# Attention block with a gated feed-forward on one core: weight preparation spaced wider, and the DMA queue reordered

## The chip, the cores and the metric

The kernel runs on one core of one Trainium2 chip. The metric is the time of one execution in device microseconds (us); lower is better. Before the change the median of three runs is 1711.38 us (1709.61 to 1713.75).

## What is computed

One transformer block in float32 with 2048 rows of 512 values. The modulation rows `sa, ca, ga, sb, cb, gb` are six slices of `silu(c) @ w_mod`.

```
h = layernorm(x) * (1 + ca) + sa
q = h @ wq  (32 heads of 16);  k = h @ wk, v = h @ wv  (one shared head of 16)
p = softmax(q @ k^T / 4);  o = p @ v
x = x + ga * (o @ wo)
h = layernorm(x) * (1 + cb) + sb
out = x + gb * (((h @ w_gate) * (h @ w_up)) @ w_down)      (inner width 1792)
```

Products whose inputs are not small are made from float16 halves: a value is scaled, rounded to float16 (the high half), and the rest is kept as a second float16 value (the low half). Three matmul terms then replace one. Each weight matrix needs a scale for that, and the scale comes from a bound on the size of its entries.

## The kernel before

**Units, turns, steps.** The attention runs in 32 units u. A unit is one block of 256 rows (eight blocks) and one group of 8 heads (four groups). It has 16 key tiles kt; the work of one kt is called a turn here. A turn has two steps, so unit u has the steps 32u to 32u+31. In a turn TensorE makes four score tiles `sc` (line 647, `qk_exp`), ScalarE turns them into `P` by exp (line 649), and TensorE adds `P` times the values into `pv` (line 658). Each turn also makes the row maxima of a unit one ahead: score tiles `mx` (line 592) whose maxima VectorE takes (line 596). VectorE and ScalarE therefore have one fixed load per turn, and four exp instructions mark one turn in the trace.

**Side work.** TensorE's remaining time in a turn goes to groups of "side" matmuls (line 502), taken in order from a list `fill`: first 16 projections of q (`q_proj`), then for each block of 256 rows the output product (`wo_work`), the gate and up products and the down product (`ffn_work`). A turn with a q projection takes in fewer side matmuls (called a thin turn here, order `FEW`) than one with later groups (a full turn, order `MANY`). Thin turns are nearly all of the steps 0 to 156 and 172 to 192; the rest are full. Which style a turn has is fixed when the program is written out, and so is the order on every engine; each engine runs its own list strictly in order.

**Weight preparation.** `late_weights` makes a list of items, and `side_step` issues one item when its gap in steps since the last one is over. `stage` loads one piece of a weight (224 or 256 KB) from HBM into one of three buffers `wsl`. `norms` squares the pieces on GpSimd and adds them up by column (`square`, lines 928 and 930); `sums` adds the columns over partitions with a matmul (line 940). `gcols` to `last_inverse` make scales from the maxima. `split` and `pipelined` load the pieces a second time, scale them on GpSimd and write the two halves (lines 1044 to 1052). The order before is: norms of `wo`, `w_gate`, `w_up`; their scales; the split of those three; norms of `w_down`; its scale; its split.

**The queue.** Nearly every DMA is issued by SyncE (SP), one after the other, and an issue that has to wait holds all behind it. The list of SP holds: the loads of weight pieces (line 921), which wait until GpSimd has released one of the three buffers; the writes of the q halves (line 540), which wait for GpSimd; the loads of a unit's q halves into `sst` (`load_q`, line 557); the row maxima `mt` of a unit (line 630), which its first score tile needs; at each unit's end (`pv_out`) eight small copies of the output `ev` to `oc` and two of the row sums to `rs` (lines 672, 674); the steps of `normalise`, that is the load `rc` of the row sums (line 682), VectorE's reciprocal (line 685), its write `ri` and its broadcast load `rr` (lines 687, 689); the rows of x for the residual (line 719).

**Normalisation.** `hooks` runs the three parts of `normalise(u - 1)` in unit u at the steps 5 (load), 10 (reciprocal on VectorE, in line with the maxima) and 15 (product and halves on GpSimd, lines 694 to 697). After every fourth unit it puts the output product and the feed-forward groups into `fill`.

Of the kernel before, what the change touches and what calls it, by code (L numbers as in the profile page):

```python
# [25 lines left out]
NC = KC  # L26
# [30 lines left out]
def adaln_mqa_glu_kernel(ctx: ExitStack, tc: tile.TileContext, x_in, wq_in, wk_in, wv_in, wo_in,  # L57
# [473 lines left out]
    def q_proj(b, ch):  # L531

        def evac(p):
            q16 = work.tile([128, 2, BT], F16, name="q16", tag="ev", bufs=3)
            qf = work.tile([128, BT], F32, name="qf", tag="ev", bufs=3)
            nc.scalar.activation(qf, p, AF.Copy, scale=qvs[:, 0:1])
            nc.gpsimd.tensor_scalar(q16[:, 0, :], qf, 1.0, 0.0, op0=OP.mult, op1=OP.add)
            nc.gpsimd.tensor_tensor(q16[:, 1, :], qf, q16[:, 0, :], op=OP.subtract)
            d = dram.tile([128, 2, BT], F16, name=f"qd{b}_{ch}")
            nc.sync.dma_start(d, q16)  # L540
# [120 lines left out]
    def pv_out(u):  # L661
        sb, ch = divmod(u, NC)
        ev = work.tile([128, BT], F32, name="ev", tag="ev", bufs=3)
        nc.scalar.activation(ev, pvb[u], AF.Copy, scale=evs)
        ps_give(pvb[u])
        oc[u] = work.tile([128, ST], F32, name="oc", tag="oc", bufs=2)
        rsum[u] = dram.tile([8, ST], F32, name=f"rs{u}")
        for c in range(2):
            for j in range(4):
                p, a = divmod(j, 2)  # L670
                r = 16 * (4 * p + 2 * c + a)
                nc.sync.dma_start(oc[u][r:r + 16, :], ev[32 * j:32 * j + 16, c * ST:(c + 1) * ST])  # L672
        for p in range(2):
            nc.sync.dma_start(rsum[u][4 * p:4 * p + 4, :].rearrange("(c a) n -> a c n", a=2),
                              ev[64 * p + 16:64 * p + 64:32, :].rearrange("a (c n) -> a c n", c=2))

    def normalise(u):
        st = {}
# [34 lines left out]
    xls = {}  # L713
    n2s = {}
    n2f = {}

    def load_x(t):
        xl = work.tile([128, D], F32, name="xl", tag="xl", bufs=3)
        nc.sync.dma_start(xl, x_rows[t * 128:(t + 1) * 128, :])
        xls[t] = xl  # L720

    def wo_work(sb):
        on_pool = 2 <= sb < NS - 2

        def op(t):
            def f(i):
                ch, term = divmod(i, 3)
                ol, wl = TERMS[term]
                return [(och[sb, ch][:, ol, t * 128:(t + 1) * 128], wo[:, wl, ch, :])]
            return f  # L730

        def fin(t):
            row = 2 * sb + t

            def f(p):
                if sb < NS - 1:
                    x1 = work.tile([128, D], F32, name="x1", tag="x1", bufs=6)
                else:
                    x1 = work.tile([128, D], F32, name="x1p", tag="P", bufs=8)
                nc.vector.scalar_tensor_tensor(x1, p, sca[:, 7:8], xls[row], op0=OP.mult, op1=OP.add)  # L740
                x1s[row] = x1
# [142 lines left out]
    def late_weights():  # L884
# [30 lines left out]
        items = []  # L915
        sl = list(wslices())
        gm = work.tile([128, 4], F32, name="gm", bufs=1)

        def stage(n):
            t = work.tile([128, D], F32, name="wsl", tag="xl", bufs=3)  # L920
# [26 lines left out]
        def norms(order):  # L947
            ns = [n for m in order for n in range(len(sl)) if sl[n][0] == m]
            out = []
            waiting = deque()  # L950
            for j in range(len(ns) + 2):
                def f(j=j):
                    if j < len(ns):
                        stage(ns[j])
                    if j >= 2:
                        square(ns[j - 2])
                out.append((SQ_GAP, nothing, f))
                if waiting:
                    out.append((0.5,) + sums(*waiting.popleft()))
                m = sl[ns[j - 2]][0] if j >= 2 else None  # L960
                if m is not None and (j == len(ns) + 1 or sl[ns[j - 1]][0] != m):
                    waiting.extend((m, n) for n in range(4))
            out.append((SUM_GAP, nothing, nothing))
            return out + [(2,) + sums(*w) for w in waiting]

        def gcols():
            nc.vector.tensor_reduce(cmx[:, 0:4], cmq, axis=AX.X, op=OP.max)
# [40 lines left out]
            nc.gpsimd.tensor_scalar(gab, gab, sca[:, 3:4], 0.0, op0=OP.mult, op1=OP.add)  # L1008

        def last_column():  # L1010
            nc.vector.tensor_reduce(cmx[:, 2:3], cmq[:, 2], axis=AX.X, op=OP.max)

        def last_scale():
            t = work.tile([128, 2], F32, name="scd", bufs=1)
# [37 lines left out]
                nc.gpsimd.tensor_tensor(wt[:, 1, i, c], t, wt[:, 0, i, c], op=OP.subtract)  # L1052
            return load, gate, halves

        def pipelined(ns):
            sp = [split(n) for n in ns]
            out = []
            for n in range(len(ns) + 2):
                def f(n=n):
                    if n >= 2:  # L1060
                        sp[n - 2][2]()
                    if n < len(ns):
                        sp[n][0]()
                    if 1 <= n <= len(ns):
                        sp[n - 1][1]()
                out.append((SPLIT_GAP, nothing, f))
# [5 lines left out]
        items += norms((2,)) + [(1, nothing, last_column), (2, tr, trp), (3, bc, last_scale), (1, nothing, last_inverse)]  # L1072
        return items, pipelined(list(range(n2, len(sl)))), [m0(k) for k in range(KC)] + [m1, m2, m3]

    def run_items(items):
        for _, f, post in items:
# [168 lines left out]
    def hooks(u, i):  # L1245
        step = u * NSTEP + i
        if later_h and i % 2 and i > 4:
            b1, k = later_h.popleft()
            h_halves(b1, (k,))
        side_step(step)  # L1250
        if u > 0 and i in (5, 10, 15):
            if i == 5:
                nrm[:] = normalise(u - 1)
            nrm[(5, 10, 15).index(i)]()
        if i == 16 and u > 0 and u % NC == 0:
            sb = u // NC - 1
            left = list(fill)
            fill.clear()
            gu, down = ffn_work(sb)
            early = max(len(left) - LATE_Q, 0) if sb == 0 else min(len(left), 2)  # L1260
            fill.extend(left[:early])
            fill.extend(([step + (6 if sb == 0 else 4)], w) for w in wo_work(sb))
            fill.extend(left[early:])
            fill.extend((["h2", sb], w) for w in gu + down)

# [77 lines left out]
```

## Time and profile before

| | |
|---|---|
| median of three runs | 1711.38 us |
| the profiled execution | 1711.02 us |
| its span, first to last instruction | 1708.9 us |
| TensorE busy | 1665.0 us (97%) |
| VectorE, ScalarE, GpSimd busy | 1404.0, 1232.1, 553.0 us |
| mean granted TensorE clock | 0.988 |
| TensorE busy from 80 to 517 us | 409.0 of 437 us, clock 0.96 |
| TensorE busy from 517 to 1600 us | 1080.7 of 1083 us, clock 1.00 |

The profiled execution takes 2.1 us more than its span and stands 0.4 us under the median. Names in the profile: PE is TensorE, PEld its weight loads, DVE VectorE, ACT ScalarE, POOL GpSimd, SP SyncE, and SPq a DMA issue on SP's queue. L596 is line 596. "A <- B" in a list of waits says that an instruction of A sat idle until B; the numbers are us in total, how many times, and the longest. In a table of windows each row is a stretch of the span, then its length, then busy us with the count of instructions, then the granted clock.

### The profile page before, as it was taken

How to read it: one execution, taken by the hardware profiler on the slowest of the kernel's cores; microseconds unless marked ns; L12 is line 12 of the kernel's file. 1: busy time of each engine (PE TensorE's matmuls, PEld its weight loads, DVE VectorE, ACT ScalarE, POOL GpSimd, SP SyncE). 2: the span in 40 equal slices, each digit the busy share in tenths (PEclk: the TensorE clock that was granted, in tenths of full speed). 3: DMA queues.
4: the chain of work that ended last, by engine and by line, in shares of the span. 5: the costliest groups of instructions: out<-in, count | busy, mean ns of one | idle time of the engine just before them, and what ended most of it. 6: DMA issues, size and time to landing. Idle time of an engine off the chain costs nothing.

```text
span 1708.9 us, 39953 instructions
## 1 busy us (share of the span) xinstructions
PE 1665.0 (97%) x15648; PEld 750.1 (44%) x15648; DVE 1404.0 (82%) x2438; ACT 1232.1 (72%) x2361; POOL 553.0 (32%) x860
## 2 busy tenths in 40 slices
PE   8988999999999999999999999999999999999999
PEld 4322232235543355434544345443545335453776
DVE  7988998789979899989999999989998999880211
ACT  5667787677867787777787777777778777787300
POOL 5766758785750111110113011310113101210322
PEclk9899999999999999999999999999999999999999
DMA  7122323331211000000000000000000000000000
GB/s 251 71 76 87 91 62 99 99 91 50 77 32 31 19 13 14 25 18 12 13 19 17 19 19 13 25 14 19 20 24 6 13 23 19 19 8 15 26 13 13
DMA packets 66024, 67.27 MB, mean 39 GB/s; under 512 B 21542, under 2 KB 50730, under 8 KB 65836
## 3 DMA queue, kind: packets, MB, share of 16 engines
q1 hardware_dynamic: 63724, 64.15, 12.4%
q8 instruction: 122, 2.00, 0.5%
q10 hardware_dynamic: 2112, 0.59, 0.1%
q14 instruction: 66, 0.54, 0.1%
HBM read 51.32 MB, written 8.92 MB: 35 GB/s over the span
## 4 chain that ended last, share of the span: by engine, by line
PE 78%; DVE 5%; POOL 4%; DMA 4%; SPq 3%; ACT 3%; issue 1%; ACTq 0%; POOLq 0%; DVEq 0%
PE side L502 35%; PE pv L658 25%; PE sc L647 9%; PE mx L592 7%; DVE mpart L596 4%; SPq L672 2%; ACT P L649 2%; DMA rc<-rs 1%; DMA rs<-ev 1%; DMA wsl<-in_B_w_up_dram 1%; POOL kwb L930 1%; PE mx L796 1%; POOL wsl L1050 1%; DMA xbig<-in_A_x_dram 1%; POOL wsl L928 0%
## 5 line engine op out<-in xcount | busy, mean ns | idle before, releaser
L596 DVE TENSOR_REDUCE mpart<-mx 128x1 f32<-128x512 f32 x2016 | 1274.1, 684 | 113.8 <-PE mx L592 98.1
L649 ACT ACTIVATE P<-sc 128x512 f32<-128x512 f32 x2048 | 1099.1, 599 | 317.5 <-PE sc L647 238.5
L647 PE MATMUL sc<-sst,kst 50*128 50x512 f16 (+1 forms) x2297 | 699.9, 357 | 9.1 <-DMA sst<-mt 5.1
L592 PE MATMUL mx<-kst,sst 48*128 48x512 f16 x2032 | 640.6, 380 | 12.8 <-DVE mpart L596 7.9
L658 PE MATMUL pv<-P,vst 128*32 128x512 f32 x4096 | 550.6, 610 | 0.6
L502 PE MATMUL side<-h2T,wg 64*128 64x256 f16 (+1 forms) x2372 | 536.5, 271 | 0.2 <-ACT P L649 0.2
L502 PE MATMUL side<-h2T,wu 64*128 64x256 f16 (+1 forms) x2372 | 534.8, 270 | 0.0
L502 PEld LDWEIGHTS <-wg 64*128 64x128 f16 (+1 forms) x2372 | 224.1, 95 | 222.3 <-ACT P L649 183.9
L502 PE MATMUL side<-wd,glu 64*128 64x512 f16 (+1 forms) x1166 | 267.7, 378 | 0.4 <-ACT P L649 0.4
L841 POOL TENSOR_SCALAR glu<-gf 128x256 f16<-128x256 f32 x112 | 45.3, 405 | 659.0 <-DVE gf L840 612.2
L647 PEld LDWEIGHTS <-kst 50*128 50x128 f16 x2297 | 209.9, 94 | 88.7 <-issue 64.8
L502 PEld LDWEIGHTS <-wu 64*128 64x128 f16 (+1 forms) x2372 | 224.4, 95 | 49.1 <-issue 12.3
L592 PEld LDWEIGHTS <-sst 48*128 48x128 f16 x2064 | 191.6, 95 | 37.0 <-issue 14.4
L502 PEld LDWEIGHTS <-glu 64*128 64x128 f16 (+1 forms) x1166 | 97.1, 95 | 194.3 <-ACT P L649 87.7
L658 PEld LDWEIGHTS pv<-P,vst 128*32 128x32 f32 x4096 | 81.1, 108 | 164.8 <-issue 154.3
L840 DVE TENSOR_TENSOR gf<-side,g 128x256 f32<-128x256 f32 x112 | 46.7, 418 | 76.6 <-ACT g L838 68.0
L502 PE MATMUL side<-h,wq 64*128 64x512 f16 (+1 forms) x372 | 99.5, 382 | 0.5 <-ACT P L649 0.4
L838 ACT ACTIVATE g<-side 128x256 f32<-128x256 f32 x112 | 42.4, 379 | 72.3 <-PE side L502 70.6
L502 PE MATMUL side<-wo,och 64*128 64x512 f16 (+1 forms) x360 | 88.0, 382 | 0.1
L694 POOL TENSOR_TENSOR oc<-oc,rr 128x256 f32<-128x256 f32 x31 | 22.6, 729 | 176.8 <-DMA sst<-qd 131.7
L842 POOL TENSOR_TENSOR glu<-gf,glu 128x256 f16<-128x256 f32 x112 | 75.3, 672 | 9.4
L502 PEld LDWEIGHTS <-och 64*128 64x128 f16 (+1 forms) x360 | 30.8, 95 | 68.7 <-ACT P L649 30.2
(230 smaller groups left out, 814.2 us busy)
## 6 DMA issues: line engine op xcount, KB each, us to landing
wsl<-in_B_w_gate_dram SPq DMA_DIRECT2D x32, 224.0 KB
wsl<-in_B_w_up_dram SPq DMA_DIRECT2D x32, 224.0 KB
wsl<-in_B_w_down_dram SPq DMA_DIRECT2D x28, 256.0 KB
sst<-qd SPq DMA_DIRECT2D x180, 32.0 KB
qd<-q SPq DMA_DIRECT2D x16, 256.0 KB
oc<-ev SPq DMA_DIRECT2D x256, 16.0 KB
rr<-ri SPq DMA_DIRECT2D x32, 128.0 KB
xl<-in_A_x_dram SPq DMA_DIRECT2D x16, 256.0 KB
```

Of the source, the lines that this page charges most:

```text
L502: return nc.tensor.matmul(self.p[:, c * w:(c + 1) * w], left[rows], right[rows], start=start and c == 0, stop=stop and c == len(terms) - 1)
L592: nc.tensor.matmul(m, s[64 * a:64 * a + 48, p, t * 128:(t + 1) * 128], w[64 * a:64 * a + 48, :], start=(i == 0), stop=(i == len(keys) - 1))
L596: nc.vector.tensor_reduce(part, m, axis=AX.X, op=OP.max)
L647: nc.tensor.matmul(t[:, c0:c1], kst[64 * a:64 * a + 50, kt * 128:(kt + 1) * 128], s[64 * a:64 * a + 50, p, c0:c1], start=True, stop=True)
L649: ex = nc.scalar.activation(ptl[u, kt, p, a], t, AF.Exp)
L658: nc.tensor.matmul(pvb[u][32 * j:32 * j + 32, :], vst[:, kt, :], ptl[u, kt, p, a], start=(kt == 0), stop=(kt == KT - 1))
L672: nc.sync.dma_start(oc[u][r:r + 16, :], ev[32 * j:32 * j + 16, c * ST:(c + 1) * ST])
L694: eng.tensor_tensor(o, o, st["r"], op=OP.mult)
L838: nc.scalar.activation(g, p[:, 0:ST], AF.Copy, scale=2.0 ** -45)
L840: nc.vector.tensor_tensor(gf, p[:, ST:2 * ST], g, op=OP.mult)
L841: nc.gpsimd.tensor_scalar(glu()[:, 0, f, :], gf, 1.0, 0.0, op0=OP.mult, op1=OP.add)
L842: nc.gpsimd.tensor_tensor(glu()[:, 1, f, :], gf, glu()[:, 0, f, :], op=OP.subtract)
```

## The change

Weight preparation:

- Squares are issued every 2.75 steps (2.0 before), splits every 2.25 steps, and every 2.0 steps for the second half of `w_gate` and `w_up` (2.0 for all before).
- A piece is squared, or scaled and split, one item after its load instead of two.
- A column sum is issued at least three items after the last square of its matrix; before, the first came with the next item.
- `w_down` has no squares on GpSimd and no column sums any more. Each of its 14 pieces is squared once on ScalarE with a running row sum (`row_norms`, line 976, every 1.5 steps), and the largest of these sums gives its bound. The bound is by rows of the piece, no longer by columns.

The queue:

- `pv_out` issues the two copies of row sums ahead of the eight copies to `oc`.
- The write of a q block's halves is issued 8 steps after its halves are begun.
- The x rows are loaded into the buffer in which the residual is then added (`x1`), no longer into one of the three `wsl` buffers.

Steps: `normalise` has its parts at 5, 12 and 18. The output product is put into `fill` at step 20 of a unit instead of 16 and may start at step 22 for the first block (as before) and at step 21 for the others (20 before); for the second block it now stands ahead of the first block's down product.

```diff
-SQ_GAP = 2.0
-SUM_GAP = 4.0
-SPLIT_GAP = 2.0
+SQ_GAP = 2.75
+ROW_GAP = 1.5
+SUM_GAP = 6.0
+SUM_LAG = 3
+SPLIT_GAPS = (2.25, 2.0)
+NORM_AT = (5, 12, 18)
+Q_LAG = 8
...
-            nc.sync.dma_start(d, q16)
             qd[b, ch] = d
+            after(Q_LAG, lambda: nc.sync.dma_start(d, q16))
...
+        for p in range(2):
+            nc.sync.dma_start(rsum[u][4 * p:4 * p + 4, :]...)
         for c in range(2):
             for j in range(4):
                 ...
                 nc.sync.dma_start(oc[u][r:r + 16, :], ev[32 * j:32 * j + 16, c * ST:(c + 1) * ST])
-        for p in range(2):
-            nc.sync.dma_start(rsum[u][4 * p:4 * p + 4, :]...)
...
+        def row_norms(ns):
+            out = []
+            for j in range(len(ns) + 1):
+                def f(j=j):
+                    if j < len(ns):
+                        stage(ns[j])
+                    if j:
+                        t = st[ns[j - 1]]
+                        nc.scalar.activation(t, t, AF.Square, accum_out=rown[:, j - 1:j])
+                out.append((ROW_GAP, nothing, f))
+            return out
...
-        items += pipelined(list(range(KC)) + by_column)
-        items += norms((2,)) + [(1, nothing, last_column), ...]
+        items += pipelined(list(range(KC)) + by_column[:16], SPLIT_GAPS[0]) + pipelined(by_column[16:], SPLIT_GAPS[1])
+        items += row_norms(range(n2, len(sl))) + [(1, nothing, last_column), ...]
...
-        if i == 16 and u > 0 and u % NC == 0:
+        if i == 20 and u > 0 and u % NC == 0:
...
-            early = max(len(left) - LATE_Q, 0) if sb == 0 else min(len(left), 2)
+            early = max(len(left) - LATE_Q, 0) if sb == 0 else int(len(left) > 2)
```

Two places show what moves. The first is SP's list around the end of unit 4. The names: `qd<-q` is a write of q halves, `sst<-mt` the row maxima that the first score tile of unit 5 needs, `xl` or `x` a load of x rows, `rs` and `oc` what `pv_out` copies. Before:

```order
L540 DMA qd_1_4446<-q_4441 128x1024
L921 DMA wsl<-in_B_w_gate_dram 128x448
L630 DMA sst_130<-mt_4459 2x8x128
L630 DMA sst_130<-mt_4460 2x8x128
L719 DMA xl<-in_A_x_dram 128x512
L921 DMA wsl<-in_B_w_up_dram 128x448 x3
L719 DMA xl<-in_A_x_dram 128x512
L672 DMA oc<-ev 16x256 x8
L674 DMA rs_4646<-ev 2x2x256 x2
```

And now, SP at the same place:

```order
L634 DMA sst_130<-mt_4382 2x8x128
L634 DMA sst_130<-mt_4383 2x8x128
L923 DMA wsl<-in_B_w_up_dram 128x448
L725 DMA x_4393<-in_A_x_dram 128x512
L923 DMA wsl<-in_B_w_up_dram 128x448 x2
L545 DMA qd_1_4375<-q_4370 128x1024
L725 DMA x_4542<-in_A_x_dram 128x512
L673 DMA rs_4569<-ev 2x2x256 x2
L679 DMA oc<-ev 16x256 x8
```

The write of the q halves stood ahead of the maxima and now stands behind them, and the row sums moved ahead of the eight copies.

The second place is the end of unit 6, first on SP before. Here the weight pieces `wsl` are those of `w_down`, `rc`, `ri` and `rr` are the steps of `normalise`:

```order
L921 DMA wsl<-in_B_w_down_dram 128x512
L630 DMA sst_129<-mt_6087 2x8x128
L630 DMA sst_129<-mt_6088 2x8x128
L672 DMA oc<-ev 16x256 x8
L674 DMA rs_6320<-ev 2x2x256 x2
L682 DMA rc<-rs_6320 128x16
L687 DMA ri_6537<-rc 128x16
```

SP at this place now:

```order
L923 DMA wsl<-in_B_w_down_dram 128x512
L634 DMA sst_129<-mt_6033 2x8x128
L634 DMA sst_129<-mt_6034 2x8x128
L923 DMA wsl<-in_B_w_down_dram 128x512 x4
L673 DMA rs_6260<-ev 2x2x256 x2
L679 DMA oc<-ev 16x256 x8
L923 DMA wsl<-in_B_w_down_dram 128x512 x2
L686 DMA rc<-rs_6260 128x16
```

The loads of `w_down` pieces stand on both sides of the ten copies: five pieces ahead, the sixth and seventh right behind.

ScalarE at the same end of unit 6, before (`P<-sc` is the exp, `g` a part of the gate product, `ev` the output copy of `pv_out`):

```order
L838 ACTIVATE g<-side 128x256
L649 ACTIVATE P<-sc 128x512 x12
L838 ACTIVATE g<-side 128x256
L664 ACTIVATE ev<-pv,evs 128x512
L649 ACTIVATE P<-sc 128x512 x12
```

ScalarE now, where `wsl,rown<-wsl` is the square of one `w_down` piece:

```order
L839 ACTIVATE g<-side 128x256
L668 ACTIVATE ev<-pv,evs 128x512
L976 ACTIVATE wsl,rown<-wsl 128x512 x2
L653 ACTIVATE P<-sc 128x512 x4
L976 ACTIVATE wsl,rown<-wsl 128x512
```

Between the exps stand squares. The two behind `ev` are those of the fifth and the sixth piece, and the sixth is the one whose load stands behind the ten copies on SP.

More of the change, by code (lines that the diff above doesn't have):

```diff
@@ L717, in load_x @@
     def load_x(t):
-        xl = work.tile([128, D], F32, name="xl", tag="xl", bufs=3)
-        nc.sync.dma_start(xl, x_rows[t * 128:(t + 1) * 128, :])
-        xls[t] = xl
+        if t < KT - 2:
+            x1s[t] = work.tile([128, D], F32, name="x1", tag="x1", bufs=6)
+        else:
+            x1s[t] = work.tile([128, D], F32, name="x1p", tag="P", bufs=8)
+        nc.sync.dma_start(x1s[t], x_rows[t * 128:(t + 1) * 128, :])
     def wo_work(sb):
@@ L735, in f @@
             def f(p):
[L736 to L741, printed above, removed]
+                x1 = x1s[row]
+                nc.vector.scalar_tensor_tensor(x1, p, sca[:, 7:8], x1, op0=OP.mult, op1=OP.add)
                 s2 = work.tile([128, 1, 2], F32, name="st2", bufs=5)
@@ L950, in norms @@
             waiting = deque()
-            for j in range(len(ns) + 2):
+            for j in range(len(ns) + 1):
                 def f(j=j):
@@ L954, in f @@
                         stage(ns[j])
-                    if j >= 2:
-                        square(ns[j - 2])
+                    if j:
+                        square(ns[j - 1])
                 out.append((SQ_GAP, nothing, f))
[L958 to L962, printed above, removed]
-            out.append((SUM_GAP, nothing, nothing))
-            return out + [(2,) + sums(*w) for w in waiting]
+                if waiting and j >= waiting[0][0]:
+                    out.append((0,) + sums(*waiting.popleft()[1:]))
+                m = sl[ns[j - 1]][0] if j else None
+                if m is not None and (j == len(ns) or sl[ns[j]][0] != m):
+                    waiting.extend((j + SUM_LAG, m, n) for n in range(4))
+            out.append((SUM_GAP, nothing, nothing))
+            return out + [(2,) + sums(*w[1:]) for w in waiting]
+        def row_norms(ns):
+            out = []
+            for j in range(len(ns) + 1):
+                def f(j=j):
+                    if j < len(ns):
+                        stage(ns[j])
+                    if j:
+                        t = st[ns[j - 1]]
+                        nc.scalar.activation(t, t, AF.Square, accum_out=rown[:, j - 1:j])
+                out.append((ROW_GAP, nothing, f))
+            return out
         def gcols():
@@ L1010, in last_column @@
         def last_column():
-            nc.vector.tensor_reduce(cmx[:, 2:3], cmq[:, 2], axis=AX.X, op=OP.max)
+            nc.vector.tensor_reduce(cmx[:, 2:3], rown, axis=AX.X, op=OP.max)
         def last_scale():
@@ L1053, in split, with pipelined @@
             return load, gate, halves
-        def pipelined(ns):
+        def pipelined(ns, gap):
             sp = [split(n) for n in ns]
             out = []
-            for n in range(len(ns) + 2):
+            for n in range(len(ns) + 1):
                 def f(n=n):
-                    if n >= 2:
-                        sp[n - 2][2]()
                     if n < len(ns):
                         sp[n][0]()
-                    if 1 <= n <= len(ns):
+                    if n:
                         sp[n - 1][1]()
-                out.append((SPLIT_GAP, nothing, f))
+                        sp[n - 1][2]()
+                out.append((gap, nothing, f))
             return out
@@ L1070, in late_weights @@
         by_column = sorted(range(KC, n2), key=lambda n: sl[n][1][1].start)
-        items += pipelined(list(range(KC)) + by_column)
-        items += norms((2,)) + [(1, nothing, last_column), (2, tr, trp), (3, bc, last_scale), (1, nothing, last_inverse)]
-        return items, pipelined(list(range(n2, len(sl)))), [m0(k) for k in range(KC)] + [m1, m2, m3]
+        items += pipelined(list(range(KC)) + by_column[:16], SPLIT_GAPS[0]) + pipelined(by_column[16:], SPLIT_GAPS[1])
+        items += row_norms(range(n2, len(sl))) + [(1, nothing, last_column), (2, tr, trp), (3, bc, last_scale), (1, nothing, last_inverse)]
+        return items, pipelined(list(range(n2, len(sl))), SPLIT_GAPS[0]), [m0(k) for k in range(KC)] + [m1, m2, m3]
     def run_items(items):
@@ L1250, in hooks @@
         side_step(step)
-        if u > 0 and i in (5, 10, 15):
-            if i == 5:
+        if u > 0 and i in NORM_AT:
+            if i == NORM_AT[0]:
                 nrm[:] = normalise(u - 1)
-            nrm[(5, 10, 15).index(i)]()
-        if i == 16 and u > 0 and u % NC == 0:
+            nrm[NORM_AT.index(i)]()
+        if i == 20 and u > 0 and u % NC == 0:
             sb = u // NC - 1
@@ L1259, in hooks @@
             gu, down = ffn_work(sb)
-            early = max(len(left) - LATE_Q, 0) if sb == 0 else min(len(left), 2)
+            early = max(len(left) - LATE_Q, 0) if sb == 0 else int(len(left) > 2)
             fill.extend(left[:early])
-            fill.extend(([step + (6 if sb == 0 else 4)], w) for w in wo_work(sb))
+            fill.extend(([step + (2 if sb == 0 else 1)], w) for w in wo_work(sb))
             fill.extend(left[early:])
```

6 lines of the change are left out of this document (3 added, 3 removed).

## The prediction

> **What bounds the kernel now.** I read the page first: the busy line, then TensorE's slices and its granted clock.
>
> ```profile
> PE 1665.0 (97%) x15648; PEld 750.1 (44%) x15648; DVE 1404.0 (82%) x2438; ACT 1232.1 (72%) x2361; POOL 553.0 (32%) x860
> PE   8988999999999999999999999999999999999999
> PEclk9899999999999999999999999999999999999999
> ```
>
> TensorE sets the pace, and what it loses lies in the first third. How much, I read from the exps of line 649 by stretch, since four of them mark a turn. Columns: stretch, length, busy us and count of exps, clock.
>
> ```profile
> 80.00:130.00 50.00, 33.24 (x65) 0.93 0.32 96
> 130.00:180.00 50.00, 33.53 (x66) 0.97 0.31 95
> 180.00:230.00 50.00, 37.89 (x74) 1.00 0.21 62
> 230.00:266.00 36.00, 28.40 (x56) 1.00 0.32 94
> 266.00:320.00 54.00, 33.99 (x65) 0.91 0.33 98
> 320.00:370.00 50.00, 33.02 (x63) 0.97 0.32 93
> 370.00:417.00 47.00, 34.62 (x66) 1.00 0.25 68
> 464.00:517.00 53.00, 35.43 (x67) 0.94 0.13 36
> 517.00:563.00 46.00, 34.17 (x64) 1.00 0.10 29
> ```
>
> Two rows serve as floors: thin turns run undisturbed from 230 to 266 us (36.00/56 = 0.643 us per exp, 1.29 us per step), full turns from 517 to 563 us (46.00/64 = 0.719 us, 1.44 us per step). What the other rows take over their floor is lost: 50 - 65 x 0.643 = 8.2 us; 7.6; 2.4; in 266 to 320 us 12.2; in 320 to 370 us, with 24 exps in full and 39 in thin turns, 7.7; in 464 to 517 us 53 - 67 x 0.719 = 4.8. Together 42.9 us. From 370 to 417 us nothing is lost.
>
> Then the waits, to see which end last there. The first four rows are from the list for the whole span, the fifth from VectorE's list for 517 to 1600 us, the sixth from SP's own list for 80 to 370 us.
>
> ```profile
> DVE rc L685 <- DMA rc<-rs: 32.2, 17, 11.9
> PEld mx L940 <- POOL kwb L928: 6.5, 1, 6.5
> PE sc L647 <- DMA sst<-mt: 5.1, 3, 3.3
> PE mx L592 <- DMA sst<-qd: 3.5, 2, 3.1
> DVE rc L685 <- DMA rc<-rs: 16.6, 10, 11.9
> SPq L540 <- POOL q L538: 72.9, 14, 11.5
> ```
>
> TensorE waits once for a column sum whose squares are late on GpSimd, and for transfers (`mt`, `qd`) that SP issued late. VectorE stands at the reciprocal for the row sums. SP stood 72.9 us at writes of q halves. The chain of waits shows the reciprocal's case around 475 us:
>
> ```profile
> 474.66 0.59 SPq L672
> 475.30 0.55 SPq L674
> 475.90 1.76 DMA rs<-ev
> 477.73 1.97 DMA rc<-rs
> 479.72 0.25 DVE rc L685
> ```
>
> Eight copies at 0.59 + 0.04 us are issued ahead of the row sums, and the reciprocal, with all maxima behind it, waits for what follows.
>
> **The change part by part.** *Sums three items later, squares every 2.75 steps.* The durations on GpSimd (min/median/max ns):
>
> ```profile
> L928 POOL TENSOR_TENSOR wsl<-wsl x40: 923/934/1042, 88.0 to 405.2; 128x448 f32<-128x448 f32 x24, 128x512 f32<-128x512 f32 x16
> L930 POOL TENSOR_TENSOR kwb<-kwb,wsl x40: 1126/1140/1277, 89.2 to 406.3; 128x448 f32<-128x448 f32 x24, 128x512 f32<-128x512 f32 x16
> L1050 POOL TENSOR_SCALAR wsl<-wsl,sca x32: 636/639/645, 256.3 to 356.8; 128x448 f32<-128x448 f32 x32
> L1051 POOL TENSOR_SCALAR wg<-wsl x16: 564/564/565, 257.0 to 346.2; 128x448 f16<-128x448 f32 x16
> L1052 POOL TENSOR_TENSOR wg<-wsl,wg x16: 1031/1036/1042, 257.7 to 346.8; 128x448 f16<-128x448 f32 x16
> L1044 POOL TENSOR_TENSOR wsl<-wsl,gab x4: 1269/1272/1276, 241.9 to 251.4; 128x512 f32<-128x512 f32 x4
> L537 POOL TENSOR_SCALAR q<-qf x16: 613/618/622, 76.8 to 362.6; 128x512 f16<-128x512 f32 x16
> L538 POOL TENSOR_TENSOR q<-qf,q x16: 1152/1158/1162, 77.5 to 363.3; 128x512 f16<-128x512 f32 x16
> ```
>
> A square with its addition takes 0.93 + 1.14 + 0.14 us between instructions = 2.2 us. At 2 thin steps (2.57 us) that fills 86% of GpSimd before the q halves; at 2.75 steps (3.54 us) 62%. The first sum moves from step 15 to 23, 8 steps or 10 us later, against a longest wait of 6.5 us: the wait goes. In 80 to 180 us I count 14.5 of 15.8 us as won.
>
> *Row sums first, reciprocal two steps later.* The two copies gain 8 x 0.63 = 5.0 us, the reciprocal comes 2.6 to 2.9 us later. What is late next is the load `rc` itself, which still stands behind all ten copies: it gains only SP's short wait for `rs`. With both, the 4.4 us that VectorE stood at 475 us are covered (2.9 + 1.7 us). I count 1.5 us in 180 to 230, 4.8 us at 475, and 3 us of the 16.6 us after 517 us, where TensorE is busy 1080.7 of 1083 us and little of it reached the path.
>
> *q halves 8 steps later, x rows in place.* The write comes 10 us after the halves were begun. SP passes it without waiting unless GpSimd lags more, so `mt` and `qd` are on time: 11 of 12.2 us in 266 to 320. The first load of such a block (unit 2's, step 18) still follows the moved write (step 8) by 10 steps, so the delay costs nothing while SP keeps within 13 us of its program. The x load no longer waits in the ring of three.
>
> *Product at step 18, output product from step 20 on.* The same matmuls in another order for the second block, the same order for the rest. The product's three GpSimd instructions are due by the fourth head group's terms, some 6 steps later; side groups of the list cover TensorE until then. I count nothing, and 1 us per block where GpSimd lags by more than those 9 us.
>
> *The splits.* Here GpSimd remains the limit. A piece of `w_gate` or `w_up` costs 0.64 + 0.56 + 1.04 + 0.21 = 2.45 us, one of `wo` 1.27 + 0.62 + 1.16 + 0.21 = 3.26 us, a q block 1.92 us. The rest of GpSimd's work is read from a stretch that has only that:
>
> ```profile
> 600.00:700.00 100.00, 99.92 (x1136) 54.27 (x1130) 92.86 (x159) 79.63 (x156) 15.39 (x29) 1.00 0.06 14
> ```
>
> Counting gaps, the splits now run from step 139 to 217: 37 thin steps x 1.29 + 41 full x 1.44 = 106.8 us. Demand: 32 x 2.45 + 4 x 3.26 + 4 x 1.92 + 15.4% of 106.8 = 115.5 us. GpSimd thus ends about 9 us after step 217, an estimate. On the way the lag is some 8 us at step 178, so a load that needs the buffer of three pieces back is up to 1 us late, and the halves of the first feed-forward input cost 0 to 1 us. I keep 5 of 7.7 us in 320 to 370 as won, and charge 1 us.
>
> *Rows of w_down on ScalarE.* Fourteen squares move to an engine on which every exp is queued behind them. Rows for one square, its accumulator, a load and an exp's surroundings:
>
> ```profile
> L409 ACT ACTIVATE wqj<-wqst x4: 617/630/638, 40.3 to 42.9; 128x512 f32<-128x512 f32 x4
> L409 ACT ACTIVATION_READ_ACCUMULATOR wqj<-wqst x4: 185/188/207, 40.8 to 43.5; 128x1 f32 x4
> 276.87 2.51 DMA wsl<-in_B_w_up_dram
> L921 SPq DMA_DIRECT2D wsl<-in_B_w_down_dram x28: 327/332/450, 354.5 to 478.2; - x28
> 517.00:563.00 46.00, 46.00 (x381) 14.09 (x373) 43.23 (x74) 35.71 (x67) 5.68 (x19) 1.00 0.10 29
> ```
>
> Work: 14 x 0.82 = 11.5 us within 20 steps (29 us), where ScalarE has 22% free, 6.4 us. Taken as busy shares that is 5 us too much; overlapping instructions make it nearer 0; I take 2. Waits: the second piece needs the buffer of the next-to-last split. GpSimd frees it at 9 - 2.5 = 6.5 us after step 217, and with 0.33 us of issue and 2.51 us of transfer it lands 9.4 us after, while ScalarE reaches its square at step 221, 5.8 us after: 3.6 us, bounds 0 and 7 with the lag's error; I take 4. The sixth piece is loaded behind the ten copies, which wait for `ev`; its square follows `ev` on ScalarE with one square between. Wait: 10 x 0.62 + 0.33 + 2.51 - 0.82 = 8.2 us. TensorE can run ahead by a few score tiles only, so I count it whole; the last pair, behind `rr`, 2 us. Sum 2 + 4 + 8 + 2 = 16 us, bounds 3 and 24.
>
> A wait is counted with no loss after it. By the Trainium skill (TensorE: Matmul & The Clock Gate, What's actually happening) an idle window of about 3.4 us halves the clock until a busy window has passed. Behind the two long waits that would be two windows, an estimate of 3.4 us more, and the time would be 1691 us. The rows of lost time show clocks of 0.91 to 0.97 where stalls stand; yet the stretch at 475 us lost 4.8 us on a wait of 4.4 us, and I go by that row.
>
> Sum: 14.5 + 1.5 + 11 + 5 + 4.8 + 3 = 39.8 us won, 1 + 16 = 17 us lost, net 22.8 us. From the profiled 1711.0 us (0.4 us under the median) I get 1688 us. The tail is covered by side groups before and after and gives nothing.
>
> **The rivals.** *Rows nearly free:* the lag is gone by step 217 and run-ahead swallows the rest; the rows cost the lower bound 3 us. For it: ScalarE's free 22%. Against: the sixth load stands behind `ev`, lag or no lag. Net 39.8 - 1 - 3 = 36 us, 1675 us.
>
> *GpSimd's backlog stays on the path:* demand still exceeds supply in the splits, so loads keep SP waiting, and the 16 us won from 266 to 370 us shrink to 2. Against: in 370 to 417 us, with GpSimd as loaded, nothing was lost. Net 9 us, 1702 us.
>
> *Every square waits for its own piece* (slower): SP gets to a load only when ScalarE has released the piece before, so each of 14 squares waits 2.84 us, 40 us, plus 5.4 us more for the sixth and 2 us of work, 47 us. Net 39.8 - 1 - 47 = -8, 1720 us. It decides where the rows cost over 38.8 us. Against: three buffers let SP issue two pieces ahead.
>
> *Stalls only move:* what SP no longer waits for, it waits for in the next load; 1711 us.
>
> *A table reload at each switch between exp and square:*
>
> ```profile
> L182 ACT ACT_TABLE_LOAD x1 | 1.3, 1283 | 2.8 <-issue 2.8
> ```
>
> The squares stand in ten groups between exps, 20 switches x 1.283 = 25.7 us, 1714 us. The row speaks against it: one load in the whole span, though squares (40.3 us) stood between exps. By the Trainium skill (ScalarE: Activation LUTs, What ACT_TABLE_LOAD costs) a switch of set costs about 2.66 us with its drain, an estimate of 53 us here and 1741 us; the page doesn't list the square with the exp's set.
>
> **How the numbers follow.** Chances: forecast 0.56, rows nearly free 0.18, backlog 0.17, every square 0.04, stalls only move 0.04, reload 0.01. The range reaches from below the free rows (7 us of unwon estimates) to the backlog case: 1668 to 1702 us. About 0.2% (3.4 us) is what a measurement of this kernel can tell from no change. Faster: 0.56 + 0.18 + 0.17 = 0.91; same, with the reload: 0.05; slower: 0.04.
>
> **What would show it.** Right: no wait of TensorE for column sums, none of VectorE for `rc` in the first eight units, SP's wait at q writes near zero; 64 exps in 41 to 43 us up to unit 3; an idle ScalarE of about 8 us behind `ev` of unit 6, released by the load of a `w_down` piece, and of some us three turns earlier. Wrong: no such gap on ScalarE (then 1675 us), waits for `mt` or `qd` between steps 140 and 200 (then 1702 us), or a gap at each square.

## The result and the profile after

The changed kernel takes 1685.74 us (median of 4 runs, 1684.02 to 1686.82); beside it the kernel before took 1712.27 us. The ratio is 0.9846 with a 95% interval of 0.9829 to 0.9863, about 26 us less. The profiled execution took 1686.8 us with a span of 1685.0 us.

The same lines of the page as before:

```profile
PE 1649.3 (98%) x15616; PEld 749.8 (44%) x15616; DVE 1402.5 (83%) x2434; ACT 1239.6 (74%) x2389; POOL 524.7 (31%) x833
PE   8999999997999999999999999999999999999999
PEclk9899999998999999999999999999999999999999
```

GpSimd is busy 28 us less and ScalarE 7.5 us more: the squares and sums of `w_down` have moved. One slice of TensorE now stands out, where before there were the third and the fourth: it is the tenth, 379 to 421 us, and its clock is lower too. To see what was won and lost at each place I divide the span by units. A unit starts where its first value product (`pv`, line 658 before, 662 after) starts. These are the exps of the kernel before in its units 0, 4, 7 and 8 (columns: stretch, length, busy us and count, clock, DMA share, GB/s):

```profile
79.90:129.80 49.90, 33.14 (x65) 0.93 0.32 96
...
265.70:320.10 54.40, 34.29 (x65) 0.91 0.33 98
...
417.50:464.30 46.80, 34.42 (x64) 1.00 0.22 63
464.30:516.70 52.40, 34.83 (x65) 0.93 0.12 36
```

And of the changed kernel in its units 0, 4, 5, 6, 7 and 8:

```profile
80.30:121.40 41.10, 32.91 (x65) 1.00 0.25 77
...
245.90:288.60 42.70, 33.27 (x65) 1.00 0.31 93
288.60:335.50 46.90, 32.44 (x63) 1.00 0.33 92
335.50:389.70 54.20, 35.65 (x66) 0.94 0.31 91
389.70:450.90 61.20, 34.39 (x64) 0.92 0.23 69
450.90:497.10 46.20, 34.66 (x65) 1.00 0.26 75
```

The work is the same (63 to 66 exps), so the lengths compare directly. Units 0 and 4 lost 8.8 and 11.7 us less. Unit 7 takes 61.2 us where it took 46.8, and unit 6 takes 54.2 where it took 47.7: there the change loses. From the end of unit 8 on, the kernel before had 1708.9 - 516.7 = 1192.2 us left, and the changed one has 1685.0 - 497.1 = 1187.9.

The waits of the changed kernel, the first four rows from the list of the whole span, the last from SP's own list for 80 to 370 us:

```profile
ACT wsl L976 <- DMA wsl<-in_B_w_down_dram: 11.4, 4, 8.7
DVE rc L689 <- DMA rc<-rs: 10.7, 1, 10.7
PE side L506 <- POOL h2T L810: 2.4, 2, 1.9
PEld L596 <- DMA sst<-qd: 1.9, 1, 1.9
SPq L545 <- POOL q L542: 3.0, 2, 2.3
```

Gone are TensorE's wait for the column sum, VectorE's waits for `rc` in the units (the one that is left lies behind the last unit) and nearly all of SP's 72.9 us at the writes of q halves. New is ScalarE's wait for pieces of `w_down`. The chain of waits at the start of unit 7 shows the longest of them:

```profile
390.61 0.59 ACT ev L668
391.21 0.54 SPq L673
...
392.36 0.59 SPq L679
...
396.78 0.59 SPq L679
397.42 2.95 DMA wsl<-in_B_w_down_dram
400.98 0.19 ACT wsl L976
...
401.70 0.40 PE mx L596
```

The ten copies go out one after the other, only then does SP issue the sixth piece, and ScalarE's square (ending at 401.17 us) holds every exp until it has landed. What that did to the clock is in the table of windows (columns: stretch, length, PE, PEld, DVE, ACT, POOL busy, clock, DMA share, GB/s):

```profile
392.00:394.00 2.00, 0.30 (x4) 0.02 (x1) 1.30 (x3) 0.00 (x0) 0.41 (x1) 1.00 0.04 12
...
395.00:396.00 1.00, 0.00 (x0) 0.00 (x0) 0.00 (x0) 0.00 (x0) 0.00 (x0) 0.63 0.07 21
396.00:401.00 5.00, 0.00 (x0) 0.00 (x0) 0.00 (x0) 0.56 (x2) 0.00 (x0) 0.50 0.47 145
...
402.00:405.00 3.00, 3.00 (x19) 0.76 (x17) 0.69 (x1) 1.83 (x5) 0.00 (x0) 0.50 0.28 87
405.00:406.00 1.00, 1.00 (x14) 0.78 (x12) 0.42 (x1) 0.70 (x2) 0.00 (x0) 0.75 0.76 254
```

TensorE stops at about 392.3 us, the clock falls to half 3.0 us later (395.3 us), and the first 3.8 us of work after the wait (401.7 to 405.5 us) run at half speed. The second new loss is at the start of unit 6. The chain there:

```profile
335.75 1.04 POOL wg L1066
336.79 0.60 POOL h2T L810
...
339.97 1.03 POOL wg L1066
341.01 0.60 POOL h2T L810
...
341.64 0.37 PE side L506
```

GpSimd makes the halves `h2T` of the first feed-forward input between two splits, in the order of its list, and TensorE's side groups stand waiting for them.

### The profile page after: what moved, and what is told of

Read it like the earlier page. It is cut to its first block, busy times and chain, and to the rows that moved or that the text cites. A ratio compares the mean times of both kernels' runs of the same rounds, so it can differ in the third digit from the quotient of the medians.

```text
span 1685.0 us, 39905 instructions
## 1 busy us (share of the span) xinstructions
PE 1649.3 (98%) x15616; PEld 749.8 (44%) x15616; DVE 1402.5 (83%) x2434; ACT 1239.6 (74%) x2389; POOL 524.7 (31%) x833
## 4 chain that ended last, share of the span: by engine, by line
PE 87%; POOL 4%; ACT 3%; DVE 2%; DMA 2%; issue 1%; SPq 1%; ACTq 0%; POOLq 0%; DVEq 0%
PE side L506 39%; PE pv L662 28%; PE sc L651 10%; PE mx L596 8%; ACT P L653 2%; DVE mpart L600 1%; SPq L679 1%; POOL wg L1066 1%; POOL wsl L1064 1%; DMA wsl<-in_B_w_down_dram 1%; DMA xbig<-in_A_x_dram 1%; PE mx L797 0%; POOL wg L1065 0%; DMA wsl<-in_B_w_up_dram 0%; PE mxt L624 0%
## 5 line engine op out<-in xcount | busy, mean ns | idle before, releaser
L841 DVE TENSOR_TENSOR gf<-side,g 128x256 f32<-128x256 f32 x112 | 46.7, 418 | 77.8 <-ACT g L839 69.1
L506 PE MATMUL side<-h,wq 64*128 64x512 f16 (+1 forms) x372 | 95.9, 376 | 0.5 <-ACT P L653 0.4
L839 ACT ACTIVATE g<-side 128x256 f32<-128x256 f32 x112 | 42.4, 379 | 72.2 <-PE side L506 70.6
```

Of the source, the lines that this page charges most:

```text
L506: return nc.tensor.matmul(self.p[:, c * w:(c + 1) * w], left[rows], right[rows], start=start and c == 0, stop=stop and c == len(terms) - 1)
L839: nc.scalar.activation(g, p[:, 0:ST], AF.Copy, scale=2.0 ** -45)
L841: nc.vector.tensor_tensor(gf, p[:, ST:2 * ST], g, op=OP.mult)
```

## Experiments

Twelve kernels, each the changed kernel with the edit shown. Four at a time ran on one chip beside the kernel before, which took 1712.66 us (e1 to e4), 1713.43 us (e5 to e8) and 1710.79 us (e9 to e12) there. Differences between kernels of different groups are therefore taken from the ratios, times 1712 us. The table has the lengths of units 0 to 9 in us, worked out from the starts of the value products in each trace:

| kernel | 0 | 1 | 2 | 3 | 4 | 5 | 6 | 7 | 8 | 9 | ratio, 95% interval |
|---|---|---|---|---|---|---|---|---|---|---|---|
| before | 49.9 | 49.8 | 43.0 | 43.1 | 54.5 | 49.6 | 47.7 | 46.8 | 52.4 | 46.5 | |
| changed | 41.1 | 41.0 | 41.2 | 42.2 | 42.7 | 47.0 | 54.2 | 61.2 | 46.2 | 48.6 | 0.9846, 0.9829 to 0.9863 |
| e1 rows later | 41.1 | 41.0 | 41.2 | 42.2 | 42.7 | 46.7 | 51.4 | 49.4 | 46.6 | 49.3 | 0.9761, 0.9746 to 0.9775 |
| e2 rows resident | 41.1 | 41.0 | 41.2 | 42.2 | 42.7 | 46.2 | 53.1 | 48.8 | 46.3 | 48.6 | 0.9759, 0.9744 to 0.9773 |
| e3 pause in splits | 41.1 | 41.0 | 41.2 | 42.2 | 42.7 | 46.9 | 47.7 | 61.7 | 50.4 | 48.6 | 0.9837, 0.982 to 0.9853 |
| e4 rows, own queue | 41.1 | 41.0 | 41.2 | 42.2 | 42.7 | 46.7 | 51.9 | 50.5 | 46.6 | 48.6 | 0.9768, 0.9754 to 0.9783 |
| e5 sums last | 41.1 | 42.6 | 42.4 | 42.6 | 43.4 | 46.2 | 54.3 | 60.3 | 46.3 | 48.6 | 0.9877, 0.9857 to 0.9896 |
| e6 q at once | 41.1 | 47.3 | 41.2 | 42.2 | 50.0 | 52.2 | 52.7 | 61.2 | 46.4 | 48.6 | 0.9948, 0.9927 to 0.9969 |
| e7 sum next | 41.7 | 41.2 | 41.3 | 42.2 | 42.7 | 44.1 | 52.6 | 61.8 | 46.3 | 48.6 | 0.9827, 0.9807 to 0.9846 |
| e8 two pauses | 41.1 | 41.0 | 41.2 | 42.2 | 42.7 | 46.5 | 47.8 | 49.1 | 46.6 | 50.5 | 0.9737, 0.9717 to 0.9757 |
| e9 both | 41.7 | 41.2 | 41.2 | 42.2 | 42.7 | 44.1 | 47.7 | 52.2 | 46.2 | 52.1 | 0.978, 0.9765 to 0.9794 |
| e10 old spacing | 42.7 | 41.7 | 43.6 | 40.7 | 42.3 | 44.7 | 55.0 | 57.1 | 46.2 | 48.6 | 0.9844, 0.983 to 0.9859 |
| e11 old spacing, sum next | 48.9 | 48.0 | 43.7 | 40.7 | 42.3 | 44.7 | 53.5 | 58.6 | 46.3 | 48.6 | 0.9918, 0.9902 to 0.9935 |
| e12 norm early | 41.1 | 41.5 | 41.5 | 42.2 | 42.7 | 46.5 | 54.0 | 59.9 | 46.3 | 48.6 | 0.9871, 0.9857 to 0.9886 |

**What the rows of `w_down` cost, and why (e1, e2, e4).** Three ways to take the load of the sixth piece out from behind the ten copies, with the squares kept on ScalarE. The first puts a pause ahead of the rows, so that no piece is loaded at a unit's end:

```diff
-        items += row_norms(range(n2, len(sl))) + [...]
+        items += [(14, nothing, nothing)] + row_norms(range(n2, len(sl))) + [...]
```

> The changed kernel with a pause of 14 steps ahead of the row squares, so that none of their loads stands behind the ten copies at unit 6's end. Theory A (ScalarE waits 8.7 us there for a load that SP issues behind the copies): the first two turns of unit 7 fall from 17.1 us to about 6, the time from 1685.7 to about 1675 us (1671 to 1678). Theory B (it is the squares' own work on a ScalarE that is 78% busy): the same work comes 14 steps later and costs as much there, 1684 to 1688 us.

The second makes the same 14 squares read a resident tile and loads nothing. It leaves out the true bound of `w_down`, so its time shows the work of the squares without their loads:

```diff
-                    if j < len(ns):
-                        stage(ns[j])
                     if j:
-                        t = st[ns[j - 1]]
-                        nc.scalar.activation(t, t, AF.Square, accum_out=rown[:, j - 1:j])
+                        nc.scalar.activation(ssqs[0][:, 0:D], gbb, AF.Square, accum_out=rown[:, j - 1:j])
```

> The fourteen squares stay where they are on ScalarE but read a tile that is resident, and the loads for them are left out; the bound of w_down is therefore not that of w_down. Theory A (waits for loads): all waits of squares go, about 1672 us (1669 to 1675). Theory B (work of the squares): 1683 to 1687 us.

The third keeps the steps of the loads, issues them from ScalarE's own queue, and squares a piece two items after its load instead of one:

```diff
-            for j in range(len(ns) + 1):
+            for j in range(len(ns) + 2):
...
-                        stage(ns[j])
+                        stage(ns[j], nc.scalar)
-                    if j:
-                        t = st[ns[j - 1]]
+                    if j > 1:
+                        t = st[ns[j - 2]]
```

> The loads of the fourteen pieces are issued on ScalarE's own DMA queue instead of SP's, and each square comes two items after its load; steps and copies as in the changed kernel. Theory A: no square waits for SP, about 1674 us (1671 to 1678), with up to 2 us for the issues on ScalarE. Theory B: 1684 to 1689 us.

Measured: 1672.65, 1671.99 and 1673.72 us. Against the changed kernel the ratios are 0.0085, 0.0087 and 0.0078 lower, 13 to 15 us, and unit 7 falls from 61.2 to 49.4, 48.8 and 50.5 us. ScalarE's wait for pieces is short in the kernel with the pause:

```profile
ACT wsl L976 <- DMA wsl<-in_B_w_down_dram: 2.0, 2, 1.2
```

So it is the wait for the load behind the copies that costs, not the work: with the loads left out, units 6 and 7 together take 101.9 us, of which 5.9 us are the stall at the start of unit 6 (turns of 7.18 and 4.80 us where before had 6.09 together); that leaves 96.0 against 94.5 us before, 1.5 us for fourteen squares. Not all of the 13 to 15 us belongs to the loads: in the kernel with the pause and in the one with its own queue the first two turns of unit 6, where neither edit has begun to act, are 1.4 and 1.0 us shorter than in the changed kernel. The last section says what differed there.

**The stall at the start of unit 6 (e3).** A pause of 6 steps between the two lists of splits lets GpSimd catch up before the halves of the first feed-forward input are due:

```diff
-        items += pipelined(..., SPLIT_GAPS[0]) + pipelined(by_column[16:], SPLIT_GAPS[1])
+        items += pipelined(..., SPLIT_GAPS[0]) + [(6, nothing, nothing)] + pipelined(by_column[16:], SPLIT_GAPS[1])
```

> The changed kernel with a pause of 6 steps between the two halves of the splits, ahead of step 190. Theory C (the 6.5 us lost in the first two turns of unit 6 are GpSimd's backlog of pieces ahead of the halves of the first feed-forward input): the two turns fall from 12.2 to about 6.5 us, the time to about 1680 us (1678 to 1683). Theory D (the halves themselves, the copy from ScalarE and the order of the groups set it): the turns stay at 12 us, 1684 to 1688 us.

Measured: 1684.79 us, not to be told from the changed kernel. By the total the backlog theory looks refuted; the units say otherwise. Unit 6 takes 47.7 us, as before the change, so its 6.5 us were GpSimd's backlog. But ScalarE's longest wait is as long as it was (8.6 against 8.7 us), and unit 8 loses 4.2 us that it hadn't lost:

```profile
ACT wsl L976 <- DMA wsl<-in_B_w_down_dram: 9.4, 2, 8.6
```

The chain of this kernel at the end of unit 8:

```profile
484.08 1.17 POOL wd L1066
...
485.26 0.33 SPq L923
...
485.68 0.59 SPq L634
...
486.37 1.69 DMA sst<-mt
...
488.11 0.39 PE sc L651
```

The pause moved the second load of `w_down` too. A load that waits for GpSimd to release a buffer now stands on SP ahead of the row maxima of unit 9, and the first score tile waits for them.

**Both at once (e8).** A pause of 6 steps in the splits and one of only 8 ahead of the rows, so that the rows and all behind them stand where the pause of 14 had put them:

```diff
-        items += pipelined(..., SPLIT_GAPS[0]) + pipelined(by_column[16:], SPLIT_GAPS[1])
-        items += row_norms(range(n2, len(sl))) + [...]
+        items += pipelined(..., SPLIT_GAPS[0]) + [(6, nothing, nothing)] + pipelined(by_column[16:], SPLIT_GAPS[1])
+        items += [(8, nothing, nothing)] + row_norms(range(n2, len(sl))) + [...]
```

> The changed kernel with the pause of 6 steps between the two lists of splits and a pause of 8 steps ahead of the rows of `w_down`; the rows and the second load of `w_down` then stand at the steps of the 14-step pause, 1672.7 us. Theory A: the two waits are separate; unit 6 loses the GpSimd wait of its first two turns (51.4 to about 47.7 us, as the 6-step pause alone did) and the end of unit 8 stays free, since the second load of `w_down` doesn't move against the 14-step pause: about 1669 us (1667 to 1671). Theory B: GpSimd's backlog is only put off, and what the pause spares at unit 6 is lost behind the later splits, in unit 6 or 7: 1671 to 1675 us.

Measured: 1667.87 us, ratio 0.9737, the fastest here: 0.0109 or 19 us below the changed kernel. Unit 6 takes 47.8, unit 7 49.1, unit 8 46.6 us; unit 9 loses 1.9 us. TensorE's stretch from 80 to 517 us in the changed kernel, then in this one (columns as in the table of windows above):

```profile
80.00:517.00 437.00, 416.88 (x3751) 160.41 (x3748) 396.70 (x685) 349.29 (x688) 269.85 (x357) 0.98 0.26 78
```

```profile
80.00:517.00 437.00, 429.10 (x3879) 164.35 (x3877) 409.23 (x705) 360.60 (x713) 273.44 (x362) 1.00 0.27 79
```

**Row sums and steps of `normalise` (e5, e12).** The first kernel undoes both, the second only the steps (the first edit of the two below):

```diff
-NORM_AT = (5, 12, 18)
+NORM_AT = (5, 10, 15)
...
-        for p in range(2):
-            nc.sync.dma_start(rsum[u][4 * p:4 * p + 4, :]...)
         for c in range(2):
...
                 nc.sync.dma_start(oc[u][r:r + 16, :], ...)
+        for p in range(2):
+            nc.sync.dma_start(rsum[u][4 * p:4 * p + 4, :]...)
```

> The changed kernel with one part undone: the two copies of row sums stand behind the eight copies to `oc` again, and `normalise` has its parts at steps 5, 10 and 15. Theory A (the prediction's): this part holds the 4.8 us won around 475 us, 1.5 us in 180 to 230 us and 3 us later, 9.3 us together; VectorE waits for `rc` again, 15 us or more over the span, and the time is about 1695 us (1691 to 1700). Theory B: the wider spacing of the weight pieces freed the queue, and the row sums are on time either way; the time stays within 2 us of 1685.7 us.

> The changed kernel with the parts of `normalise` at steps 5, 10 and 15 again, the row sums still first on the queue. With both undone the time was 1692.6 us. Theory A: the two copies of row sums, 5.0 us earlier on the queue, carry the gain; the load `rc` still stands behind all ten copies, but the steps cost nothing: 1684 to 1687 us. Theory B: since `rc` stands behind the eight copies in either order, it is the two steps (2.6 to 2.9 us) that cover VectorE's wait: 1690 to 1693 us, and VectorE waits for `rc` 8 us or more beyond the 10.7 us of the changed kernel.

Measured: 1692.6 us for both undone, 1688.31 us for the steps alone; the ratios are 0.0031 and 0.0025 above the changed kernel, 5.3 and 4.3 us, with intervals that overlap. VectorE's waits for `rc` separate the two better. Both undone, then the steps alone (12.1 us of the first and 10.9 us of the second are one wait behind the last unit, as are the 10.7 us of the changed kernel):

```profile
DVE rc L689 <- DMA rc<-rs: 20.6, 13, 12.1
```

```profile
DVE rc L689 <- DMA rc<-rs: 15.2, 8, 10.9
```

Neither theory of the second kernel holds whole: the order of the copies counts (3.9 us lost in units 1 to 4 of the first kernel against 0.8 in the second), and so do the steps (8 waits in place of 1). From the end of unit 8 on, the two kernels take 3.0 and 3.3 us more than the changed one; what they have in common is the old steps. Neither brings back what unit 8 had lost: 46.3 us in both. So the old order and the old steps aren't enough for that loss of the kernel before, which the prediction tied to this part. SP's list of before for 455 to 490 us shows what came on top, loads of `w_down` that waited for GpSimd ahead of the copies:

```profile
SPq L921 <- POOL wd L1052: 13.8, 6, 3.8
```

In the kernel before, ScalarE was done with `ev` at 465.7 us, but SP stood at four of these loads until 469.85 us and issued the first copy at 469.9, 4.3 us later. In the kernel with both undone `ev` ends at 454.7 us and the first copy is issued at 454.7: SP was waiting for it, and VectorE doesn't wait for `rc` in that unit. Whether the new order alone would have removed the loss in the kernel before was not tried.

**The late write of q halves (e6).**

```diff
-            after(Q_LAG, lambda: nc.sync.dma_start(d, q16))
+            nc.sync.dma_start(d, q16)
```

> The changed kernel with the write of the q halves issued at once, as before, and all else kept. Theory A (the prediction's): the late write is what cleared the queue in 266 to 320 us; SP waits for GpSimd at the writes again (before: 72.9 us in 14 waits), `mt` or `qd` come late in units 4 and 5, and 8 to 11 us come back: about 1695 us (1692 to 1698). Theory B: the wider spacing of squares and splits already keeps GpSimd's lag short, so the writes wait 2 us or less each and nothing that TensorE needs is late: 1685 to 1688 us.

Measured: 1704.38 us, ratio 0.0102 or 17.5 us above the changed kernel: more than either theory gave. The waits from 80 to 370 us, the last row from SP's own list:

```profile
PE sc L651 <- DMA sst<-mt: 7.6, 2, 3.8
PE mx L596 <- DMA sst<-qd: 5.6, 1, 5.6
SPq L545 <- POOL q L542: 98.0, 15, 11.8
```

Units 1, 4 and 5 lose 6.3, 7.3 and 5.2 us; unit 6 is 1.5 us shorter. The chain at the end of unit 1 is the mechanism in four rows: the q halves are done, SP is free, the maxima go out and the score tile starts.

```profile
157.44 1.16 POOL q L542
...
158.62 0.33 SPq L545
...
159.70 1.58 DMA sst<-mt
...
161.41 0.58 PE sc L651
```

**Spacing of squares and lag of the column sum (e7, e10, e11).** Three kernels: the lag alone undone (e7, the first edit), the spacing alone undone (e10, the second edit), both undone (e11, both edits). In the last two a pause of 36.25 steps ahead of the splits keeps splits and rows where they stood, to within one step.

```diff
-SUM_LAG = 3
+SUM_LAG = 0
```

```diff
-SQ_GAP = 2.75
+SQ_GAP = 2.0
...
-        items += pipelined(list(range(KC)) + by_column[:16], SPLIT_GAPS[0]) + ...
+        items += [(36.25, nothing, nothing)] + pipelined(list(range(KC)) + by_column[:16], SPLIT_GAPS[0]) + ...
```

> The changed kernel with the first column sum issued with the item after the last square of its matrix, as before, and the spacing of 2.75 steps kept. Theory A (the prediction's): the wait for the column sum goes because the sum comes later; undone, TensorE waits for GpSimd at the sum again, 3 to 6.5 us, and the time is 1689 to 1693 us. Theory B: at 2.75 steps, 3.5 us, a piece's 2.2 us of GpSimd are done before the next item, so no backlog stands ahead of the sum and the spacing alone took the wait: 1684 to 1687 us, TensorE's wait for the sum under 1 us.

> The changed kernel with the squares every 2.0 steps again, the late column sum kept, and a pause of 36 steps ahead of the splits, so that splits and rows stand where they stood. Theory A: the spacing of the squares is what won units 0 and 1; at 2.0 steps GpSimd is 86% filled with squares before the q halves, is late with the sums even three items on, and units 0 and 1 lose 3 to 9 us: 1689 to 1695 us. Theory B: the late sum and the late write of q halves each cover the backlog, so that the old spacing costs nothing: 1684 to 1687 us.

> As the old spacing of squares, and the column sum at the next item too; the late write of q halves and all else are kept. Theory A: spacing and late sum stand in for each other, so with neither TensorE waits for the sum as before (6.5 us) and unit 0 takes 47 to 50 us again instead of 41.1: 1691 to 1695 us. Theory B: what units 0 and 1 had lost came from the writes of q halves on the queue alone; unit 0 stays under 43 us and the time is 1684 to 1688 us.

Measured: 1683.4, 1683.49 and 1696.73 us; the first two lie half a us under the ranges of theory B, the third 1.7 us over that of theory A. Each undone alone costs nothing in the total (ratios 0.9827 and 0.9844 beside 0.9846); both undone cost 0.0072 or 12 us, and units 0 and 1 take 48.9 and 48.0 us, 14.8 us more. TensorE's wait for the sum from 80 to 200 us with the lag undone, then from 80 to 180 us with both undone:

```profile
PEld mx L942 <- POOL kwb L930: 1.4, 2, 1.1
```

```profile
PEld mx L942 <- POOL kwb L930: 6.0, 1, 6.0
```

So spacing and lag stand in for each other for most of this wait. Neither is quite free where it stands: with the lag undone units 0 and 1 take 0.8 us more, with the spacing undone units 0 to 2 take 4.7 us more. The totals hide it, since units 5 and 6 are 2.9 and 1.6 us shorter in the first and the units 3, 5 and 7 are 1.5, 2.3 and 4.1 us shorter in the second. What exactly shortens those wasn't traced; the splits stand up to one step elsewhere in both.

**The pauses and the earlier sum together (e9).** The two edits of e8 and the first of the two just shown.

> The two pauses of 6 and 8 steps together with the column sum at the next item. The rows of `w_down` stand at steps 233 to 253, as with the two pauses alone (1667.9 us). Theory A: what the sum at the next item won (unit 5 in 44.1 us where it had 47.0) has its own place, a few steps of the queue in unit 5, and adds to the pauses: about 1665 us (1663 to 1667). Theory B: the gain was the same GpSimd backlog seen earlier, which the pauses already relieve: 1667 to 1670 us.

Measured: 1672.62 us, ratio 0.978 against 0.9737 of the pauses alone: a miss of both theories. Unit 5 keeps its 44.1 us, as the first theory said, but unit 7 takes 52.2 and unit 9 52.1 us, 3.1 and 1.6 us more than with the pauses alone. Behind the sums the two programs differ only in that the later items stand at most two steps earlier, so a shift of that size is enough. The two profiled executions differ by 3 us from unit 0 on, the ratios by 7; the rest isn't placed.

## Why the prediction was right, and which of its steps were not

The forecast was 1688 us and the time is 1685.74 us; the net of the sum was 22.8 us, and the profiled spans differ by 1708.9 - 1685.0 = 23.9 us. The lengths of the units give the terms.

- **Column sums, units 0 and 1:** 14.5 us predicted, 8.8 + 8.8 = 17.6 measured. The mechanism is shown: undoing spacing and lag together brings back 14.8 us and a wait of 6.0 us. The step that gave the win to the later sum was too narrow, since the spacing alone does nearly the same, and unit 1 needs the late write of the q halves too: with that alone undone it takes 47.3 us.
- **Units 2 and 3:** 1.5 us predicted, 1.8 + 0.9 = 2.7 measured; undoing the order of the copies and the steps brings back 1.2 + 0.4 = 1.6.
- **Late write of q halves, unit 4:** 11 us predicted, 11.8 measured (54.5 to 42.7). Undoing it brings back 7.3 us in this unit, so 4.5 us of the term came from elsewhere; no run tells which part gave them (the wider splits and the x rows in place are left, and the x rows were not undone by themselves). In total undoing it costs 17.5 us, more than the term, since it also stalls units 1 and 5.
- **Splits, unit 5:** 5 us predicted, 2.6 measured (49.6 to 47.0); a load of `qd` is still late there (1.9 us), which was one of the signs named for the backlog.
- **475 us, unit 8:** 4.8 us predicted, 6.2 measured. The size came out near, the reason was only part of it: with the old order and the old steps unit 8 stays at 46.3 us, since the copies no longer start 4.3 us behind `ev`.
- **Later units:** 3 us predicted; from the end of unit 8 on, 1192.2 - 1187.9 = 4.3 us measured, tail included. Undoing the steps brings back 3.0 to 3.3 us of it, so this term held. Unit 9 is 2.1 us longer than before, unit 10 2.4 us shorter; why wasn't traced.
- **First feed-forward input, unit 6:** this is the term that failed. I had GpSimd some 8 us behind at step 178 and still charged 0 to 1 us for the halves; the first two turns of unit 6 lost 7.06 + 5.16 - 6.09 = 6.1 us, and the pause in the splits took all of it away. A lag that is worked out for an engine has to be charged to the next reader of its results unless that reader has slack, and TensorE's side groups had none.
- **Rows on ScalarE:** 16 us predicted; 13 to 15 us come back when the load is moved or left out. The wait for the sixth piece was put at 8.2 us and is 8.7; the work at 2 and is 1.5; the last pair at 2 and is 2.6 (the seventh turn of unit 7, 5.49 against 2.84 us; with `normalise` two steps earlier the long turn is the sixth, 4.03 us, so it hangs on those steps); the second piece at 4 and is 1.2 (the fourteenth turn of unit 6, 4.25 against 3.06 us).
- **No loss after a wait:** this step failed too. The first two turns of unit 7 lost 12.93 + 4.18 - 6.11 = 11.0 us on a wait of 8.7. The 3.8 us at half clock make 1.9 us of the rest. By the Trainium skill (TensorE: Matmul & The Clock Gate, What's actually happening) an idle window of about 3.4 us halves the clock; the trace agrees that the clock halves, but here 3.0 us after the stop. The page's rule gave an estimate of 3.4 us for two such waits, 1691 us; the second half-clock window stood in unit 6 (340.7 to 347.5 us), not behind the second piece. The row that I went by, 4.8 us lost around 475 us on a wait of 4.4, understated the loss: unit 8 took 52.4 us where 46.2 are enough, 6.2 us, at a clock of 0.93.

What was won came out 5 us above the prediction (45.2 against 39.8 us), and what was lost (6.5 us in unit 6 and 14.4 in unit 7, and a start 0.4 us later) 4 us above it (21.3 against 17). That the two misses cancel is luck; the total is nearer to the forecast than its terms are.

Of the rivals, *rows nearly free* is false for the change, but true of the squares once their loads don't stand behind the copies. *Backlog* holds for 6 us of unit 6. *Every square waits* falls: ScalarE waits 4 times in 14. *Stalls only move* is what the pause in the splits did by itself. The *reload* falls by one row of the changed kernel:

```profile
L186 ACT ACT_TABLE_LOAD x1 | 1.3, 1283 | 2.8 <-issue 2.8
```

## What to carry to other kernels

When work moves to an engine, follow its loads first: fourteen squares cost 1.5 us of work and some 13 us more, 11 of them in the two turns behind one load that stood behind ten copies on an in-order queue. When a total doesn't move, divide the span by units of equal work before calling a theory wrong: one pause removed 6.5 us and added 4.2 elsewhere, and a second pause of the right length kept the first gain. Two edits that each cover the same wait need separate and joint undoing, since each alone looks worthless.

## What the runs showed of the hardware

TensorE's clock fell to half without a long stop. From 337.2 to 340.6 us of the changed kernel it was busy about half of the time, and when the clock fell it had stood for 0.9 us (since 339.7 us):

```profile
337.20:340.60 3.40, 1.65 (x18) 1.18 (x18) 1.92 (x4) 2.05 (x4) 3.15 (x5) 1.00 0.30 87
340.60:340.80 0.20, 0.00 (x0) 0.00 (x0) 0.20 (x1) 0.00 (x0) 0.20 (x1) 0.61 0.00 0
```

A chain of short waits can so cost clock as one long wait does; here 5.8 us of work (341.64 to 347.47 us) ran at half speed, 2.9 us of the 6.1 that the two turns lost. The rest is three waits for `h2T`, 0.5, 0.6 and 1.9 us.

The clock did not change at just any time. In the changed kernel it fell at 340.65, rose at 347.47, fell at 395.26 and rose at 405.50 us; these lie 2, 14 and 3 times 3.413 us apart. In each of the fourteen traces the changes of the clock between 60 us and the last instruction lie whole multiples of 3.413 us apart. So one stall can cost different amounts: the kernel with resident rows and the one with its own queue have the same three waits at the start of unit 6 (0.6, 0.6 and 1.9 us), but the clock was at half for 6.8 us in the first and for 3.4 us in the second (as in the kernel with the pause), and the two turns took 12.0 and 11.3 us.
